# One written list for a fused attention and gated unit: VectorE turns q and k for four heads at once, the gated unit works on 512 tokens, the last 64 tokens go in 64-column halves

## The chip, the core and the metric

The kernel runs on one core of a Trainium2 chip. The core has a matrix engine (TensorE, "PE" in the profile, with its weight loads as "PEld"), three elementwise engines (VectorE "DVE", ScalarE "ACT", GpSimd "POOL"), a queue engine for transfers (SyncE "SP") and sixteen DMA engines. On-chip data lies in SBUF, with 128 partitions. Matmul results lie in PSUM, which this kernel uses as eight banks of 128 partitions by 512 fp32 values. Each engine works through its own list of instructions in order and waits at semaphores for the others. The metric is the time of one execution on the device in microseconds (us); the profile page gives the span from the first to the last instruction of one execution.

## What is computed

Two stages follow one another. The first is block-causal attention over 8 batches, 8 heads, 576 tokens and 64 dims (blocks of 64 tokens, nine of them). The second is a gated unit over the 512 channels that the heads make together.

```python
# q, k, v: (8, 8, 576, 64) fp32
scores = matmul(q, k^T) / sqrt(64);  keep where query block >= key block (blocks of 64)
x      = softmax(scores) @ v                      # then (8, 576, 512)
gate_pre[s] = sum_k conv_w[k] * x[s - 4 + k]      # five taps for each channel, causal
val  = x @ w_val                                  # 512 x 512
out  = (sigmoid(gate_pre) * val) @ w_out          # (8, 576, 512) fp32
```

The kernel takes exp without subtracting the maximum, gets each softmax sum from a column of ones beside v, and takes the sigmoid as (1 + tanh(g/2))/2, with the factor 1/2 put into w_val.

## The kernel before, in words

**Order of work.** The order is written out by hand: `PLAN` is a list of words, and `run` calls one helper for each word, so the order of the words is the order of every engine's instructions. A word such as `s.8.1@72` names a helper (`s` is `scores`), its arguments and, behind the `@`, the PSUM banks that it writes or the engine that it runs on. A short `START` list and some set-up code (ones, zeros, identity, the Exp table) come ahead of it.

**Attention.** The unit is a pair of two heads, 32 pairs in all. Of its 576 tokens the first 512 go one way and the last 64 (the tail) another.
- `load_qk` (L194) brings q and k of a pair, 256 KB each, in runs of four tokens; `load_v` brings v; `load_tails` brings the 64 tail tokens of q and k of all heads of a batch. Nearly all loads and stores are on SP's queue.
- `cast_qk` (L231) makes fp16 of q and k on GpSimd. `trans` (L263) turns them on TensorE, eight transposes of 128 x 128 for a pair, into one PSUM bank. `evac_trans` (L276) copies the bank to SBUF on VectorE and puts the tokens in order. `trans_tails` (L285) and `evac_tails` (L290) do the same for the tails.
- `scores` takes three steps `t` for a pair. In each step the two heads sit in partitions 0 to 63 and 64 to 127 of the array (64 dims each) and write 512 columns each into one bank per head. The last 64 queries are columns of step 2 with `ktails` as moving data. `exps` (L315) empties one bank, that is 512 columns, into fp16 `pts` on ScalarE. `scores_last` and `exps_last` (L327) do the tail keys of a batch. `mask` (L332, L334) zeroes the 64 x 64 blocks that the mask forbids, on GpSimd.
- `av` has one bank for a head: five query blocks of 128 (the last block has 64 real queries beside columns that are not used), each the sum over its key blocks, with `pts` as weights and v (with its column of ones) as moving data: 15 matmuls of 65 columns. `norm` (L357, L358) divides on VectorE. `xtrans` (L365) makes five transposes for a pair, and `evac_x` (L371) writes 576 tokens into `xts`.

**Gated unit.** The unit is half a batch, 288 tokens, 16 in all. `conv` makes 80 matmuls of 32 x 32 weights (the taps as diagonals `DG`), in sixteen positions of the array, into four banks; `gate` (L388) takes tanh of one bank at a time; `val` makes four products of four matmuls with 288 columns; `gated` (L402) multiplies. `proj` makes one 128-token row block of `out` from four matmuls of 512 columns (36 in all, nine for two batches), and `evac_out` (L243) copies it to `osb` on VectorE or ScalarE before `store` sends it. The last row block is split in two halves over two engines and two queues.

All matmuls but the transposes go through one helper, so their line is L133; the tiles tell them apart: `qkT` and `kt` are scores, `v,pt` and `v16t,pt` the product with v, `xt,DG` the convolution, `xt,w_val` val, `w_out,gv` proj, `ident,qk` the transposes of q and k, `ident,x` those of x.

Of the kernel before, what the change touches and what calls it, by code (L numbers as in the profile page):

```python
# [9 lines left out]

START = """
Lqk.0
"""

PLAN = """
cw@0 Lt.0 Lqk.1 Lqk.2 cq.1 cq.0 ct.0 cT w@1 w@1 w@1 w@1 w@1 w@1 w@1 w@1 tr.0@12 qkT.0 ttr.0@3 Lt.1
Lqk.3 kt.0 qka.0 Lvt.0 cq.2 w@4 w@4 s.0.0@45 e.0.0.1 s.0.1@67 e.0.0.0 s.0.2@01 Lv.0 e.0.1.0 sl.0@23
e.0.2.0 Lqk.4 w@4 tr.1@4 qkT.1 w@5 w@5 tr.2@5 Lv.1 el.0.1 e.0.1.1 ct.1 el.0.0 s.1.1@67 e.0.2.1 qkT.2
s.1.2@23 e.1.1.1 cq.3 e.1.1.0 s.1.0@40 ttr.1@1 e.1.2.1 Lqk.5 Lv.2 Lv.3 e.1.2.0 Lqk.6 w@5 s.2.1@56
Lwv.0 cvt.0 e.1.0.0 kt.1 e.1.0.1 s.2.0@71 Lwv.1 m.0 Lqk.7 w@2 tr.3@2 qkT.3 cv.0 s.2.2@30 Lt.2  # L20
e.2.1.0 e.2.0.0 m.1 cq.4 e.2.1.1 av.0.0@4 DG e.2.0.1 e.2.2.1 av.0.1@2 s.3.2@56 n.0.1 e.2.2.0 n.0.0
e.3.2.1 cv.1 s.3.1@17 e.3.2.0 tr.4@2 s.3.0@03 m.2 av.1.1@4 qkT.4 av.1.0@5 cq.5 cv.2 xtr.0@6 n.1.1
e.3.1.0 e.3.1.1 Lvt.1 s.4.0@21 e.3.0.0 Lv.4 e.3.0.1 s.4.1@74 xt.0 Lv.5 n.1.0 tr.5@6 s.4.2@03 e.4.0.1
m.3 e.4.0.0 av.2.1@5 e.4.2.1 e.4.2.0 av.2.0@1 Lqk.8 cv.3 qkT.5 n.2.1 s.5.0@26 n.2.0 e.4.1.1 e.4.1.0
cq.6 e.5.0.0 av.3.1@0 n.3.1 e.5.0.1 Lqk.9 wv.3@P av.3.0@3 Lv.7 wv.2@P xtr.1@5 sl.1@47 Lv.6 cq.7
el.1.1 el.1.0 n.3.0 s.5.1@10 xtr.2@2 xt.1 e.5.1.1 xtr.3@6 xt.2 ct.2 tr.6@3 Lqk.11 m.4 xt.3 qkT.6
e.5.1.0 Lqk.10 s.5.2@47 Lwo.3 wv.1@D cvt.1 cn.0@5260 e.5.2.1 e.5.2.0 s.6.1@13 val.0.3@4 th.0.2 cv.4
th.0.3 Lwo.2 gv.0.3 val.0.2@7 th.0.1 m.5 th.0.0 cv.5 e.6.1.1 Lwo.0 s.6.0@02 e.6.1.0 s.6.2@56 wv.0@D
tr.7@4 val.1.2@1 ttr.2@3 e.6.2.1 gv.0.2 Lwo.1 e.6.2.0 val.0.0@7 e.6.0.0 e.6.0.1 val.0.1@5 qkT.7 cq.8
s.7.1@64 gv.0.0 e.7.1.1 s.7.0@02 e.7.1.0 m.6 av.4.1@7 e.7.0.1 Lt.3 kt.2 gv.0.1 av.4.0@3 n.4.1 cq.9  # L30
s.7.2@54 e.7.0.0 e.7.2.0 av.5.1@6 n.4.0 av.5.0@7 n.5.1 Lvt.2 n.5.0 e.7.2.1 Lv.9 m.7 sl.2@02 Lv.8
xtr.4@3 el.2.1 xt.4 val.1.3@6 el.2.0 tr.8@4 cv.7 cn.1@5702 th.1.2 th.1.3 qkT.8 th.1.1 xtr.5@3 cv.6
xt.5 Lqk.13 tr.9@4 th.1.0 val.1.0@3 s.8.0@02 Lqk.12 gv.1.2 av.7.1@1 cq.11 av.6.1@5 qkT.9 e.8.0.1
gv.1.0 n.7.1 Lv.10 cq.10 s.9.2@74 wo.1@P wo.0@P e.8.0.0 s.9.1@30 n.6.1 e.9.2.0 e.9.2.1 gv.1.3
av.7.0@2 val.1.1@1 av.6.0@5 s.8.2@64 e.9.1.0 ct.3 e.9.1.1 cvt.2 n.7.0 Lqk.14 s.8.1@72 Lv.12 n.6.0
e.8.2.0 xtr.7@0 e.8.2.1 gv.1.1 e.8.1.1 xt.7 xtr.6@3 tr.11@5 s.9.0@14 xt.6 e.8.1.0 qkT.11 e.9.0.0
Lvt.3 Lv.11 tr.10@6 cn.2@0327 e.9.0.1 qkT.10 th.2.2 s.11.0@51 cv.9 val.2.2@4 o.0.1@6 gv.2.2 th.2.0
val.2.1@4 e.11.0.1 th.2.3 th.2.1 e.11.0.0 s.10.2@02 m.8 s.10.0@37 ttr.3@1 cv.8 e.10.2.1 gv.2.1
val.2.0@5 Lt.4 kt.3 e.10.0.0 e.10.2.0 o.0.0@4 Lqk.16 oc.0.1@D m.9 sl.3@10 s.10.1@26 e.10.0.1 Lqk.15
e.10.1.0 val.2.3@3 gv.2.0 el.3.1 av.8.0@5 cq.13 av.8.1@7 gv.2.3 e.10.1.1 n.8.0 n.8.1 av.9.1@3 cq.12  # L40
el.3.0 s.11.2@26 s.11.1@01 oc.0.0@D e.11.1.1 n.9.1 tr.13@5 av.9.0@7 o.0.3@4 e.11.1.0 xtr.8@0 n.9.0
xt.8 cv.10 e.11.2.1 m.10 e.11.2.0 m.11 tr.12@1 cn.3@3726 Lqk.17 qkT.12 cq.14 av.10.1@0 oc.0.3@A
Lv.15 o.0.4@4 th.3.2 tr.14@1 cv.11 th.3.0 Lv.14 qkT.13 th.3.1 th.3.3 n.10.1 qkT.14 oc.0.4@A
s.13.0@52 s.12.0@36 e.13.0.0 av.10.0@7 n.10.0 e.12.0.1 o.0.2@4 Lqk.18 s.13.1@01 e.13.0.1 cq.16
s.12.1@25 ct.4 av.11.1@7 e.12.0.0 av.11.0@3 oc.0.2@D Lvt.4 e.13.1.1 e.12.1.1 Lv.13 xtr.10@6 xtr.9@4
n.11.1 xt.10 e.13.1.0 val.3.2@7 s.13.2@01 e.12.1.0 n.11.0 st.0.0 cq.15 e.13.2.1 s.12.2@62 e.13.2.0
e.12.2.0 Lt.6 gv.3.2 e.12.2.1 cvt.3 cv.12 xt.9 xtr.11@5 xt.11 val.3.0@3 ttr.4@7 cn.4@4015 gv.3.0
val.4.0@3 th.4.0 m.12 st.0.1 val.3.1@2 th.4.1 kt.4 th.4.2 gv.4.0 tr.15@7 sl.4@63 cv.15 th.4.3 gv.3.1
Lt.5 s.14.1@01 qkT.15 el.4.0 el.4.1 s.14.2@45 val.4.2@2 av.12.1@3 val.3.3@6 e.14.1.1 Lqk.19 Lqk.20
cq.17 e.14.2.0 av.12.0@7 gv.4.2 e.14.2.1 e.14.1.0 s.14.0@24 n.12.1 gv.3.3 st.0.2 s.15.0@53 n.12.0  # L50
s.15.1@60 st.0.3 val.4.1@1 Lv.16 m.13 tr.17@7 e.14.0.0 cv.14 e.14.0.1 gv.4.1 cv.13 xtr.12@2 tr.16@4
e.15.0.0 e.15.1.1 e.15.0.1 e.15.1.0 qkT.17 xt.12 o.0.5@1 s.15.2@35 oc.0.5@D cq.18 cn.5@7062 e.15.2.1
qkT.16 e.15.2.0 th.5.3 m.14 av.13.1@1 Lv.17 Lv.19 av.13.0@3 th.5.2 val.5.1@5 n.13.1 s.16.2@41 th.5.0
th.5.1 e.16.2.1 e.16.2.0 s.16.1@02 Lqk.22 e.16.1.0 n.13.0 s.16.0@67 m.15 gv.5.1 st.0.4 av.15.1@3
av.15.0@5 xtr.13@1 n.15.1 cq.19 ct.5 val.5.0@4 Lqk.21 e.16.1.1 av.14.0@3 n.15.0 av.14.1@0 cq.20
xtr.15@2 gv.5.0 e.16.0.0 s.17.0@54 Lvt.5 e.16.0.1 s.17.1@67 n.14.0 n.14.1 val.4.3@3 xt.15 xtr.14@0
gv.4.3 e.17.0.0 tr.19@2 xt.14 cv.16 xt.13 e.17.0.1 val.5.3@4 e.17.1.0 tr.18@5 ct.6 cv.17 qkT.18
# [52 lines left out]
def kernel(  # L110
# [10 lines left out]
    nc = tc.nc  # L121
# [7 lines left out]
    NU = B // 2  # L129
# [387 lines left out]
```

## Time and profile before

| | |
|---|---|
| time of three runs | 194.16, 195.87 (median), 196.45 us |
| span of the profiled execution (its device time is not given apart from it) | 191.6 us |
| TensorE busy | 177.3 us, 93% of the span |
| VectorE busy | 136.3 us, 71% |
| ScalarE busy | 135.8 us, 71% |
| GpSimd busy | 86.7 us, 45% |
| moved by DMA | 40.43 MB, mean 211 GB/s |
| granted TensorE clock | 0.995 over the span |

A busy time is the union of an engine's instructions. A matmul's row is longer than the time that it keeps others out, because matmuls overlap: what a group of matmuls costs the engine is the distance from its start to the start of the next group. In a group row, "xN" is the number of instructions, the numbers behind the first bar are busy time in us and mean length of one in ns, and behind the second bar stands the idle time ahead of them with what ended it.

### The profile page before, as it was taken

To read this page: it belongs to the slowest core of one execution; us is meant where nothing else is said; L and a number is where in the kernel's file an instruction comes from. 1 tells how busy PE (TensorE), PEld (TensorE's weight loads), DVE (VectorE), ACT (ScalarE), POOL (GpSimd) and SP (SyncE) were. 2 spreads that over 40 slices of the span, in tenths; PEclk is the share of its full clock that TensorE was granted. 3 is DMA by queue.
4 is the path that set the end of the run, shared out by engine and by line. 5 is a ranking of instruction groups with operands and counts; after the bars stand their busy time and mean duration, and the time that the engine had idled before them with its cause. 6 is when DMAs were issued, how large, how long until landed. Compare 5 with 4: busy or idle time off the path is not lost.

```text
span 191.6 us, 8757 instructions
## 1 busy us (share of the span) xinstructions
PE 177.3 (93%) x3687; PEld 124.7 (65%) x3687; DVE 136.3 (71%) x297; ACT 135.8 (71%) x295; POOL 86.7 (45%) x171
## 2 busy tenths in 40 slices
PE   0988899999799999999998999999999999999991
PEld 0554676777558587687576676667676777875540
DVE  6325998889738987888979765967678877762630
ACT  3059999868957788884683995978788879443432
POOL 7262889963277377445447044602469061100000
PEclk9999999999999999999999999999999999999997
DMA  6999999934589999899999887999902700300756
GB/s 168 301 310 299 317 256 285 271 97 129 135 234 308 240 287 261 220 280 227 273 263 260 270 237 197 300 209 311 307 9 86 227 30 0 113 7 0 266 205 244
DMA packets 70321, 40.43 MB, mean 211 GB/s; under 512 B 48133, under 2 KB 64773, under 8 KB 70282
## 3 DMA queue, kind: packets, MB, share of 16 engines
q1 hardware_dynamic: 69328, 39.33, 71.4%
q8 instruction: 29, 0.48, 1.1%
q10 hardware_dynamic: 954, 0.53, 0.9%
q14 instruction: 10, 0.08, 0.1%
HBM read 30.42 MB, written 9.44 MB: 208 GB/s over the span
## 4 chain that ended last, share of the span: by engine, by line
PE 73%; DMA 11%; POOL 4%; DVE 4%; ACT 2%; SPq 2%; issue 2%; ACTq 0%; POOLq 0%; DVEq 0%
PE B L133 62%; DMA w_st<-in_moe_w_out_dram 7%; PE B L263 6%; PE B L365 4%; DVE qkT L276 2%; ACT pt L315 2%; DMA conv_nat<-in_moe_conv_w_dram 2%; DMA out_dram<-osb 2%; SPq L194 1%; POOL qk L231 1%; SPq L220 1%; POOL w_val L251 1%; PE B L285 1%; DVE DG L441 1%; POOL w_out L243 1%
## 5 line engine op out<-in xcount | busy, mean ns | idle before, releaser
L315 ACT ACTIVATE pt<-B 128x512 f16<-128x512 f32 x192 | 99.5, 619 | 18.5 <-PE B L133 14.6
L231 POOL CAST qk<-qks 128x1024 f16<-128x1024 f32 x31 | 32.2, 1045 | 23.6 <-DMA qks<-in_k_dram 21.5
L276 DVE COPY qkT<-B 128x1024 f16<-128x1024 f16 x31 | 37.5, 1219 | 6.7 <-PE B L263 6.5
L402 DVE SCALAR_TENSOR_TENSOR gv<-th,B 128x288 f16<-128x288 f32 x64 | 28.0, 450 | 19.2 <-PE B L133 10.0
L133 PE MATMUL B<-xt,w_val 128*128 128x288 f16 x256 | 39.4, 287 | 0.2
L133 PE MATMUL B<-w_out,gv 128*128 128x512 f16 x144 | 35.3, 379 | 1.3 <-POOL w_out L243 1.3
L133 PEld LDWEIGHTS <-pt 128*128 128x128 f16 x960 | 33.1, 97 | 5.1 <-issue 2.6
L133 PE MATMUL B<-v,pt 128*128 128x65 f16 x896 | 35.2, 194 | 0.6 <-POOL v L234 0.3
L358 DVE TENSOR_TENSOR x<-B,rc 128x320 f16<-128x320 f32 x64 | 31.5, 492 | 2.2
L388 ACT ACTIVATE th<-B 128x288 f32<-128x288 f32 x64 | 21.5, 427 | 11.9 <-PE B L133 11.9
L332 POOL MEMSET pt<- 64x384 f16 x32 | 13.6, 424 | 35.7 <-ACT pt L315 34.8
L133 PE MATMUL B<-qkT 64*128 64x128 f16 (+3 forms) x256 | 28.9, 300 | 0.5 <-DVE qkT L276 0.4
L133 PEld LDWEIGHTS <-w_val 128*128 128x128 f16 x256 | 22.4, 98 | 8.2 <-issue 2.4
L133 PEld LDWEIGHTS <-qkT 64*128 64x128 f16 x512 | 15.1, 94 | 13.2 <-issue 5.7
L234 POOL CAST v<-vst 128x512 f16<-128x512 f32 x32 | 20.2, 639 | 7.3 <-DMA vst<-in_v_dram 4.5
L133 PEld LDWEIGHTS <-gv 128*128 128x128 f16 x144 | 13.2, 98 | 13.2 <-issue 1.5
L263 PE MATMUL B<-ident,qk 128*128 128x128 f16 x256 | 20.2, 222 | 0.8 <-DVE x L358 0.7
L263 PEld LDWEIGHTS <-qk 128*128 128x128 f16 x256 | 16.3, 99 | 5.6 <-issue 3.6
L243 ACT COPY osb<-B 128x512 f32<-128x512 f32 x19 | 11.2, 593 | 12.0 <-PE B L133 11.2
L133 PE MATMUL B<-xt,DG 32*32 32x288 f16 x1280 | 17.3, 288 | 0.9 <-issue 0.9
L357 DVE RECIPROCAL rc<-B 128x5 f32<-128x5 f32 x64 | 12.0, 188 | 8.2 <-PE B L133 7.5
L133 PEld LDWEIGHTS <-DG 32*32 32x32 f16 x1280 | 12.0, 88 | 5.7 <-issue 3.3
(51 smaller groups left out, 136.4 us busy)
## 6 DMA issues: line engine op xcount, KB each, us to landing
out_dram<-osb SPq DMA_DIRECT2D x35, 256.0 KB, 3.5
qks<-in_q_dram SPq DMA_DIRECT2D x32, 256.0 KB, 4.0
vst<-in_v_dram SPq DMA_DIRECT2D x64, 128.0 KB, 4.2
qks<-in_k_dram SPq DMA_DIRECT2D x31, 256.0 KB, 4.5
tlst<-in_q_dram SPq DMA_DIRECT2D x8, 128.0 KB, 5.7
vtst<-in_v_dram SPq DMA_DIRECT2D x8, 128.0 KB, 4.7
w_st<-in_moe_w_val_dram SPq DMA_DIRECT2D x2, 512.0 KB
w_st<-in_moe_w_out_dram SPq DMA_DIRECT2D x4, 256.0 KB
```

Source lines behind the costliest of these rows:

```text
L133: nc.tensor.matmul(out=out, lhsT=lhsT, rhs=rhs, start=start, stop=stop, skip_group_check=True)
L231: nc.gpsimd.tensor_copy(out=o, in_=s)
L234: nc.gpsimd.tensor_copy(out=v16s[p % NV][0:128, 0:4, 0:2, 0:64], in_=vst[p % NVS][0:128])
L243: (eng.copy if eng is nc.scalar else eng.tensor_copy)(out=o, in_=i)
L263: nc.tensor.transpose(out=f16(m[i * (len(m) - 1)])[:, o:o + 128], in_=t[0:128, c, 2 * i:2 * i + 2, 0:64], identity=ident16[0:128, 0:128])
L276: nc.vector.tensor_copy(out=o[0:128].rearrange("p i (s n) -> p i s n", n=4), in_=f16(m[0]).rearrange("p (i n s) -> p i s n", i=2, n=4))
L315: nc.scalar.activation(out=pts[p % NPT][0:128, h, 512 * t:512 * t + 512], in_=f32(bank["s", p, t][h]), func=AF.Exp, bias=0.0, scale=0.125)
L332: nc.gpsimd.memset(pt[64:128, 0:2, 0:1536].rearrange("p h (t s) -> p h t s", t=3)[:, :, :, 0:64], 0.0)
L357: nc.vector.reciprocal(out=rc[0:128], in_=O[:, :, 64:65])
L358: nc.vector.tensor_tensor(out=x16[p % NX16][0:128, 0:5, h, 0:64], in0=O[:, :, 0:64], in1=rc[0:128].to_broadcast([128, 5, 64]), op=ALU.mult)
L388: nc.scalar.activation(out=ths[n % NTH][0:128, r, 0:288], in_=f32(bank["cn", n][r])[:, 0:288], func=AF.Tanh, bias=0.0, scale=0.5)
L402: nc.vector.scalar_tensor_tensor(out=gvs[u % 2][0:128, x, bi, hf, 0:288], in0=ths[n % NTH][0:128, x, 0:288], scalar=1.0, in1=f32(bank["val ...
```

## The change

- **q and k** are loaded for four heads of a batch (a "quad" `Q`, 16 in all) and all 576 tokens at once: partition 32h + s holds 18 tokens of head h, 4608 bytes in one run. The cast to fp16 (GpSimd, mostly) puts two tokens side by side (`[n, d, 2]`: the pair of fp16 values is one 32-bit word), so it writes with a step of two elements. `turn` then lets VectorE transpose 32 x 32 blocks of 32-bit words, SBUF to SBUF: 576 words per partition in one instruction, written with a step of nine words. No transposes of q, k on TensorE, no copy out of PSUM, no separate tails of q, k. The first quad is cast and turned in two parts.
- **Scores**: each head holds 32 partitions, the 64 dims come as two halves that are summed in PSUM; a step writes 512 columns for four heads into four banks, as two passes of four matmuls with 32-row weights. `exps` takes two banks (1024 columns) at once. The tail queries are columns of the same tiles.
- **av** has two banks for a pair and four query blocks for a head, 20 matmuls; `norm` takes both heads at once. **The tail** is worked out once for a batch: `av_tail` puts two heads in the two 64-column halves of the array, 40 matmuls with 64-column weights; `norm_tail`, `xtrans_tail`, `evac_xtail` follow.
- **Gated unit**: 512 tokens of a batch at once (units 0 to 7), and two units (8, 9) of 256 tokens from the tails of four batches each; tanh takes two banks at once. x lies in one tile `X` with six slots. Each unit has its own row blocks in `proj` (still 36).
- **w_out** is loaded as it lies and put in order by sixteen matmuls (`wp`) and two copies (`we`), in place of loads in rearranged runs.
- **One list**: `START` and the set-up code become words of `PLAN`; casts carry their engine in the word. PSUM is one tile of eight banks. The last row block is not split.

The core of the diff:

```diff
-    qks = ring(NQS, [128, 2, 2, 256], fp32, "qks")
-    qkT = ring(NQT, [128, 2, 512], fp16, "qkT")
-    pts = ring(NPT, [128, 2, 1664], fp16, "pt")
+    stage = [ring(NST, [128, 9, 2, 64], fp32, t) for t in ("qst", "kst")]
+    half = [ring(N16, [128, 9, 64, 2], fp16, t) for t in ("q16", "k16")]
+    qTs = ring(NT, [128, 2, 576], fp16, "qT")
+    kTs = ring(NT, [128, 2, 640], fp16, "kT")
+    pts = ring(NPT, [128, 4, 1536], fp16, "pt")
...
+    def load_q(Q, m, i=0):
+        b, g = divmod(Q, 2)
+        eng = nc.scalar if m == "A" else nc.sync
+        eng.dma_start(out=stage[i][Q % NST][0:128].rearrange("p n e d -> p (n e d)"),
+                      in_=(q, k)[i][b, 4 * g:4 * g + 4].rearrange("h (p t) d -> (h p) (t d)", t=18))
...
+    def cast_qk(Q, i, m, part=(0, 9)):
+        a, e = part
+        copy(ENG[m], half[i][Q % N16][0:128, a:e].rearrange("p n d e -> p n e d"),
+             stage[i][Q % NST][0:128, a:e])
...
-    def trans(p, m):
-            for c in range(4):
-                nc.tensor.transpose(out=f16(m[i * (len(m) - 1)])[:, o:o + 128], ...
-    def evac_trans(p, m, parts=(0, 1)):
+    def turn(Q, i, m, part=(0, 9)):
+        a, e = part
+        src = half[i][Q % N16][0:128, a:e].rearrange("p n d e -> p n (d e)").bitcast(fp32)
+        dst = (qTs, kTs)[i][Q % NT][0:128, 0:2, 0:576].bitcast(fp32)
+        nc.vector.transpose(out=dst.rearrange("p h (s n) -> p n h s", n=9)[:, a:e],
+                            in_=src.rearrange("p n (h s) -> p n h s", h=2))
...
+    def score(Q, m, work, o=0):
+        qt, kt = qTs[Q % NT], kTs[Q % NT]
+        for (c, j, a, e) in work:
+            for dh in range(2):
+                for h in range(4):
+                    hp = slice(32 * h, 32 * h + 32)
+                    mm(f32(m[h])[:, o + c:o + c + e - a], kt[hp, dh, 128 * j:128 * j + 128],
+                       qt[hp, dh, a:e], start=(dh == 0), stop=(dh == 1))
+
+    WORK = [[(0, 0, 0, 512)], [(0, 1, 128, 576), (448, 4, 512, 576)],
+            [(0, 2, 256, 576), (320, 3, 384, 576)]]
...
-    def exps(p, t, h, m):
+    def exps(Q, t, h, m):
+        i, j = bank["s", Q, t][2 * h:2 * h + 2]
+        nc.scalar.activation(out=pts[Q % NPT][0:128, 2 * h:2 * h + 2, 512 * t:512 * t + 512],
+                             in_=two(i, j), func=AF.Exp, bias=0.0, scale=0.125)
...
+    def av_tail(b, m):
+        bank["at", b] = m[0]
+        for g in range(2):
+            Q = 2 * b + g
+            for h in range(2):
+                c = 65 * (2 * g + h)
+                for j in range(5):
+                    for r in range(2):
+                        a = 2 * r + h
+                        if j == 0:
+                            l = pt3[b % 2][0:128, 2 * a + g]
+                        else:
+                            l = pts[Q % NPT][0:128, a, off[j] + 512:off[j] + 576]
+                        w = v16t[b % 2][0:128, 4 * g + a, 0:65] if j == 4 else \
+                            v16s[(2 * Q + r) % NV][0:128, j, h, 0:65]
+                        mm(f32(m[0])[64 * r:64 * r + 64, c:c + 65], l, w,
+                           start=(j == 0), stop=(j == 4))
...
-                    mm(f32(m[row])[cs, 0:288], DG[rs, 5 * g + kk, 0:32],
-                       xts[b % NX][rs, g, kk + 288 * hf:kk + 288 * hf + 288],
+                    mm(psv(f32(m[row])[cs], n), DG[rs, 5 * g + kk, 0:32], tokens(n, rs, g, kk),
                        start=(kk == 0), stop=(kk == 4))
...
+    def gate(n, h, m):
+        i, j = bank["cn", n][2 * h:2 * h + 2]
+        w = width(n)
+        nc.scalar.activation(out=ths[...][0:128, 2 * h:2 * h + 2, 0:w], in_=two(i, j)[:, :, 0:w],
                              func=AF.Tanh, bias=0.0, scale=0.5)
```

Two stretches of the new list, its start and its end:

```
Lv.1.0 Lq.0@A wz pads padk Lk.0 cb.0.1@P cb.0.0@D w@0 w@0 w@0 id Lq.1 w@0 w@0 Lk.1 Lk.2 w@0 w@0 w@0
...
o.9.0@4 o.9.1@0 oc.7.0@A o.7.2@6 st.7.0 oc.7.1@D st.7.1 oc.9.0@D st.9.0 oc.9.1@D st.9.1 oc.7.2@A
st.7.2
```

More of the change, by code (lines that the diff above doesn't have):

```diff
@@ L182 @@
     bank = {}
     def f32(i):
[L185 removed]
+        return PS[0:128, i]
     def f16(i):
[L188 to L203 removed]
@@ L413, in evac_out @@
[L413 to L427 removed]
+        w = width(n)
@@ new lines @@
+    OPS = {
+        "Lq": load_q, "Lk": load_k, "Lv": load_v, "Lvt": load_vtail, "Lwv": load_w_val,
+        "Lwo": load_w_out, "Lcw": load_conv, "c": cast_qk, "ca": cast_qk_a, "cb": cast_qk_b,
+        "cv": cast_v, "cvt": cast_vtail, "wv": scale_w_val, "wo": cast_w_out, "wp": order_w_out,
+        "we": evac_w_out, "T": turn, "Ta": turn_a, "Tb": turn_b, "s": scores, "e": exps,
+        "sl": scores_last, "el": exps_last, "m": mask, "av": av, "n": norm, "xtr": xtrans,
+        "xt": evac_x, "at": av_tail, "nt": norm_tail, "xtt": xtrans_tail, "xtl": evac_xtail,
+        "cn": conv, "th": gate, "val": val, "gv": gated, "o": proj, "oc": evac_out,
+        "st": store, "cw": taps, "cT": evac_taps, "DG": diags, "w": warm, "wz": zero_wz,
+        "tab": table, "id": identity, "pads": pads, "padk": pad_k,
+    }
```

563 lines of the change are left out of this document (246 added, 317 removed).

## The prediction

> **What bounds the kernel now.** I read the busy shares first, then the busy times by stretch, then the time line of TensorE. From the page:
>
> ```profile
> PE 177.3 (93%) x3687; PEld 124.7 (65%) x3687; DVE 136.3 (71%) x297; ACT 135.8 (71%) x295; POOL 86.7 (45%) x171
> ...
> PE 73%; DMA 11%; POOL 4%; DVE 4%; ACT 2%; SPq 2%; issue 2%; ACTq 0%; POOLq 0%; DVEq 0%
> ```
>
> TensorE has 93% of the span and 73% of the chain that ended last. The next view gives length, busy time (and count) of PE, PEld, DVE, ACT, POOL, clock, DMA share and GB/s for four stretches; behind it, pieces of the chain of waits at both ends of the run (start, length, what).
>
> ```profile
> 10.00:20.00 10.00, 8.55 (x116) 5.54 (x114) 4.60 (x6) 7.96 (x17) 4.93 (x9) 1.00 1.11 302
> 20.00:40.00 20.00, 19.02 (x435) 14.53 (x432) 18.12 (x41) 19.22 (x43) 16.89 (x26) 1.00 0.94 265
> ...
> 60.00:160.00 100.00, 98.49 (x2228) 71.13 (x2226) 78.81 (x170) 79.29 (x175) 48.28 (x90) 1.00 0.79 222
> 160.00:186.50 26.50, 26.50 (x476) 17.07 (x473) 14.93 (x39) 12.60 (x29) 1.11 (x4) 1.00 0.28 102
> ```
> ```profile
> 4.65 5.36 PE B L133 x16
> 10.01 0.85 PE B L263 x8
> ...
> 169.03 17.44 PE B L133 x248
> ...
> 186.50 0.44 DVE olast L243
> ```
>
> Real work on TensorE starts at 10.0 us (dummy matmuls before), ends at 186.5, and 5.1 us of last copies and stores follow. From 60 us on TensorE is full while VectorE and ScalarE have a fifth of their time free. From 20 to 40 ScalarE is as full as TensorE (19.2 of 20). So: TensorE bounds, with ScalarE beside it early.
>
> What a matmul group costs is the distance to the next start on the time line:
>
> ```profile
> 48.10 0.61 PE L263 MATMUL B<-ident,qk 128*128 128x128 f16 x8
> 48.65 0.39 PE L133 MATMUL B<-qkT 64*128 64x512 f16 x2
> 48.97 0.62 PE L263 MATMUL B<-ident,qk 128*128 128x128 f16 x8
> 49.52 1.05 PE L133 MATMUL B<-xt,DG 32*32 32x288 f16 x80
> 50.50 0.39 PE L133 MATMUL B<-qkT 64*128 64x512 f16 x2
> ...
> 54.39 0.28 PE L133 MATMUL B<-kt,qkT 64*128 64x64 f16 x8
> 54.51 0.38 PE L133 MATMUL B<-qkT 64*128 64x512 f16 x2
> 54.82 0.40 PE L285 MATMUL B<-ident,tl 128*128 128x128 f16 x4
> 55.05 0.65 PE L133 MATMUL B<-xt,w_val 128*128 128x288 f16 x4
> 55.54 0.81 PE L133 MATMUL B<-w_out,gv 128*128 128x512 f16 x3
> ```
> ```profile
> 59.92 0.59 PE L133 MATMUL B<-v,pt 128*128 128x65 f16 x14
> 60.35 0.19 PE L133 MATMUL B<-v16t,pt 128*128 128x65 f16 x1
> 60.38 1.02 PE L133 MATMUL B<-w_out,gv 128*128 128x512 f16 x4
> 61.24 0.44 PE L365 MATMUL B<-ident,x 128*128 128x128 f16 x5
> 61.52 0.61 PE L263 MATMUL B<-ident,qk 128*128 128x128 f16 x8
> ```
>
> Four proj matmuls of 512 columns take 60.38 to 61.24, 0.86: 0.215 each. Five transposes take 0.28: 0.056 each. Eight would be 0.45, but the eight ahead of a score step or a convolution take 0.55 (48.10 to 48.65): leaving full-array work for tiles costs some 0.1, and so does the way back, since a step of 512 columns takes 0.32 (48.65 to 48.97), not 0.215. The two heads of a step run side by side (both within that 0.32). Fifteen matmuls of av take 0.46: 0.029 to 0.03 each. A convolution takes 0.98, four val matmuls 0.49, eight score matmuls of 64 columns 0.12 (54.39 to 54.51).
>
> **TensorE, part by part** (both switches counted with the tiled work).
> - Transposes of q, k: 32 x 0.45 + 8 x 0.22 = 16.2 before (54.82 to 55.05 is a tail group), nothing after.
> - Scores: before 96 steps x (0.215 + 0.2) = 39.8. After 48 steps, each two passes of 512 columns by four heads: 48 x (0.43 + 0.2) = 30.2. Tail keys: 16 matmuls at 0.015 to 0.02 a batch plus switches, 0.5; 4 after, 2.6 before.
> - av: 960 x 0.029 = 27.8 before; 640 x 0.029 = 18.6 after, plus the tail. No row shows 64-column weights; bounds are 0.0145 each (two halves side by side) and 0.058 (half the pace of the full ones). I take the row itself, 0.029: 8 x (40 x 0.029 + 0.2) = 10.9 (6.2 to 20.2).
> - Transposes of x: 160 x 0.056 = 9.0, then 144 x 0.056 = 8.1.
> - Convolution: 16 x (0.98 + 0.1) = 17.3. After, five rounds with 224 columns more, 0.094 each: 8 x 1.55 + 2 x 1.0 = 14.4.
> - val 64 x 0.49 = 31.4, then 128 x 0.215 + 32 x 0.108 = 31.0. proj 31.0 both. Taps and the ordering of w_out: 1.5.
>
> Before: 175, against the 176.5 between 10.0 and 186.5, so the method accounts for the run. After: 150. The cover of the moved set-up words (ones, zeros, identity, the Exp table) is the wait for the first loads, up to 10.0 us, as now.
>
> **The other engines.** Rows of the view by group:
>
> ```profile
> L315 ACT ACTIVATE pt<-B 128x512 f16<-128x512 f32 x192 | 99.5, 619 | 18.5 <-PE B L133 14.6 <-POOL pt L334 1.0 <-issue 0.9
> ...
> L276 DVE COPY qkT<-B 128x1024 f16<-128x1024 f16 x31 | 37.5, 1219 | 6.7 <-PE B L263 6.5
> ...
> L231 POOL CAST qk<-qks 128x1024 f16<-128x1024 f32 x31 | 32.2, 1045 | 23.6 <-DMA qks<-in_k_dram 21.5 <-PE B L133 1.6
> L358 DVE TENSOR_TENSOR x<-B,rc 128x320 f16<-128x320 f32 x64 | 31.5, 492 | 2.2
> L402 DVE SCALAR_TENSOR_TENSOR gv<-th,B 128x288 f16<-128x288 f32 x64 | 28.0, 450 | 19.2 <-PE B L133 10.0 <-ACT th L388 6.9 <-ACT pt L315 2.0
> ...
> L388 ACT ACTIVATE th<-B 128x288 f32<-128x288 f32 x64 | 21.5, 427 | 11.9 <-PE B L133 11.9
> ...
> L234 POOL CAST v<-vst 128x512 f16<-128x512 f32 x32 | 20.2, 639 | 7.3 <-DMA vst<-in_v_dram 4.5 <-PE B L133 1.8
> ...
> L371 DVE COPY xt<-B 128x576 f16<-128x576 f16 x32 | 13.9, 450 | 1.3 <-PE B L365 0.7 <-ACT pt L315 0.5
> ...
> L332 POOL MEMSET pt<- 64x384 f16 x32 | 13.6, 424 | 35.7 <-ACT pt L315 34.8
> ...
> L357 DVE RECIPROCAL rc<-B 128x5 f32<-128x5 f32 x64 | 12.0, 188 | 8.2 <-PE B L133 7.5 <-ACT pt L315 0.3
> ...
> L243 ACT COPY osb<-B 128x512 f32<-128x512 f32 x19 | 11.2, 593 | 12.0 <-PE B L133 11.2 <-ACT olast L243 0.5
> L243 DVE COPY osb<-B 128x512 f32<-128x512 f32 x16 | 10.9, 688 | 5.9 <-DMA out_dram<-osb 2.9 <-PE B L133 2.9
> ...
> L334 POOL MEMSET pt<- 64x128 f16 x32 | 6.4, 200 | 0.0
> ...
> L327 ACT ACTIVATE pt<-B 128x256 f16<-128x256 f32 x16 | 5.9, 408 | 0.5 <-PE B L133 0.5
> ...
> L251 POOL TENSOR_SCALAR w_val<-w_st 128x512 f16<-128x512 f32 x2 | 3.0, 1500 | 0.0
> ```
>
> - ScalarE: 512 columns occupy it for 99.5/192 = 0.518, and 256 more columns add (619 - 408) = 0.211, so 1024 occupy it for 0.94. 96 exps 90.2, 16 of 256 columns 4.9, 16 + 4 gates 17.1, two copies of w_out 2, 13 output copies 6.5: 121.
> - VectorE: a turn is 576 words. The copy at L276 reads PSUM with a step of 128 elements at 1.04 ns an element plus 0.15; so 0.755, 30 whole turns and two in parts, 24.2. Its writes have a step of 36 bytes, which no row shows: up to twice per element, 1.355. norm 32 x (0.19 + 0.69), tails 5 + 2.3, xt 32 x 0.42, gated 32 x 0.68 + 8 x 0.42, 23 output copies 15.9, the rest 4: 118.
> - GpSimd: 1152 elements from 639 and 1045: 1.15 a cast, 28 of them 32; v 20.4, v tails 5, masks 17, weights 8: 84. The step of two elements in the write is not in the trace; bounds 1.15 and, at the 2.93 ns an element of L251 (1500/512), 3.37. I take 1.15, the same operation.
>
> **The sum.** Up to the last exp of the sixth quad the list holds 38 us for ScalarE (36 exps of 0.94, six of 0.31, two gates), but for TensorE only 26: 18 steps 11.3, eight av 4.6, two tails 2.7, seven transposes of x 1.6, tail keys 1.5, one convolution 1.55, two val 1.7, the taps 0.9. The gated unit starts no earlier. The loads that this stretch needs are 7.1 MB of q and k, 3.1 of v, 2.1 of weights and the tails, near 13 MB: 45 us at 290 GB/s, between the 302 and 265 of the two early stretches above. So two limits lie near 48 us after a start at 10, which I leave where it is: the first quad loads twice the bytes, but no transposes and copies stand ahead of its scores. I take 49. SP has 32 loads of q and k where there were 79 with the tails, in one queue with the stores; a store that waits for its copy still holds the loads behind it, as now, so I cost it at nothing; if loads came late the stretch at 265 GB/s would be 49 us long, not 45.
>
> Then 124 on TensorE, and 5.1 for the last copy and store, plus 0.2 as the last block isn't split (0.593 for a whole copy in place of the 0.44): 178. That TensorE waits no more after 49 us is what the trace shows now; but the seventh quad holds some 10 us on each of four engines, for which I add 1. Behind the last exp, av of the last two pairs waits for a mask of 1.07 (768 and 256 elements by the slope from 200 to 424 ns at L334 and L332) that was 0.62; ahead of it in TensorE's order stand one av, three val or proj and four transposes, 3.4 us, against 1.98 + 1.07 for exps and mask: covered by 0.3. Span 179. The median run lies 4.3 above the profiled span (195.87 - 191.6), the lowest 2.6: **179 + 4 = 183**. What no longer counts is the copy at L276; what is late next is ScalarE early, then TensorE again.
>
> [...]
> [...]
>
> **Rivals.**
> - *The turn costs 1.355.* VectorE goes to 137 and is the fullest in a few quads (13 in the seventh): taking the fullest engine quad by quad, the sum rises by 6.6. **190**. Chance 0.13.
> - *PSUM banks (slower).* A step now takes four of eight banks at once and ScalarE gives them back in two pairs, the last 1.98 us after the step (1.04 + 0.94); before, two banks after 0.62 + 0.52 = 1.14. TensorE works in order: a group behind the step whose bank is not free stops everything. Price: the 0.8 difference at half of 48 steps, 20 us: **203**. It undoes the change from 0.27 a step on (13/48). For it: no row has such steps. Against it: from 60 to 160 us PE lost 1.5 of 100. Chance 0.11.
> - *GpSimd's casts at 3.37.* 62 us more, 146 in all, the fullest engine in nine quads, which adds 25 if it can run ahead and 35 if not: **208 to 218**. Chance 0.06.
> - *The change does not do what it says:* four heads run three at a time (0.43 x 4/3, 0.14 x 48 = 6.9 more: **190**, chance 0.05) or two (0.43 x 48 = 20.6 more: **203**, chance 0.03).
> - *Better:* tail matmuls two at a time (-4.7) and loads no slower than ScalarE in the first quads (-1), the seventh quad without loss (-1): **176**. Chance 0.10.
>
> **How the numbers follow.** Forecast 0.52, 178 to 188. No change of under 1% (about what a measurement of this kernel can tell, 194 to 198) lies only at the foot of the slow cases: 0.04. Slower by more: 0.19. Faster: 0.77. The range reaches from the better case, less 6 for the error of the stretch up to 49 us (half of the 12 by which ScalarE exceeds TensorE there), to the bank rival: 170 to 203; what is left out is the GpSimd case and the far ends.
>
> **What would show it.** Right: no `ident,qk` group; turns near 0.76; exps of 1024 columns near 1.04; a score step 0.6 from start to start; 40 tail matmuls in about 1.3; TensorE busy near 160, ScalarE near 121. Wrong: idle time of PE released by ACT or DVE (banks), GpSimd busy over 110 (casts), turns over 1.2, or the last exps later than 150 us.

## The result: slower by a third

The changed kernel takes 258.82 us (median of four, 258.46 to 261.28) against 196.03 us for the kernel before (194.16 to 196.45): ratio 1.340, 95% interval 1.325 to 1.354. The forecast was 183 us with a range of 170 to 203. For each set of runs below the kernel before was run again beside it; ratios are to that kernel, both without the executions that ran some per cent slower at a lower clock, while medians and ranges hold all executions.

Busy times, the chain that ended last, and the clock in 40 slices, from the page of the changed kernel (span 257.1 us, its own run 258.83 us):

```profile
PE 188.5 (73%) x3015; PEld 106.1 (41%) x3015; DVE 129.3 (50%) x232; ACT 128.1 (50%) x150; POOL 90.2 (35%) x127
...
PEclk9855556757999997799958979995558999769999
...
PE 45%; ACT 14%; DVE 14%; issue 4%; POOL 1%; ACTq 0%; DVEq 0%
PE PS L103 42%; ACT pt L271 10%; DVE x L329 5%; PE PS L343 3%; DVE gv L406 2%; DVE osb L197 2%; ACT th L388 2%; DVE rc L328 1%; DVE kT L244 1%; POOL w_val L223 1%; DVE qT L244 1%; ACT w_out L197 1%; ACT pt L281 1%; DVE X L349 0%; PE PS L354 0%
```

No engine is full. TensorE stands for 27% of the span where it stood for 7%, and the other engines are half idle. This is not an engine that has too much to do: the chain goes back and forth between TensorE, the exps (L271) and the norm (L329). The granted clock, 0.995 on average before, is 0.826.

Groups of the same kernel, shapes kept apart (line, engine, operation, count, busy us, mean ns, idle before):

```profile
L271 ACT ACTIVATE pt<-PS 128x1024 f16<-128x1024 f32 x96 | 94.0, 1023 | 67.7 <-PE PS L103 51.5 <-DVE x L329 6.3 <-DVE gv L406 4.7
...
L197 POOL CAST k<-kst 128x1152 f16<-128x1152 f32 x14 | 20.6, 1479 | 9.2 <-DVE gv L406 5.9 <-DVE kT L244 3.1
...
L244 DVE STREAM_TRANSPOSE qT<-q 128x576 f32<-128x576 f32 x15 | 18.1, 1209 | 3.0 <-POOL q L197 2.9
L244 DVE STREAM_TRANSPOSE kT<-k 128x576 f32<-128x576 f32 x15 | 18.1, 1204 | 0.0
```

The exps are as long as forecast (1.02 us); turn and cast are longer (1.21 and 1.48 us). But look at the idle time of the exps: ScalarE waits 6.3 us for the norm and 4.7 us for the gated product, both VectorE's work. An exp needs nothing from either of them. So these waits look like waits for a place, not for a result, and PSUM is the place that an exp, a norm and a gated product share.

The waits of the changed kernel (us in total, times, longest):

```profile
PEld L103 <- issue: 86.7, 152, 3.0
ACT pt L271 <- PE PS L103: 51.5, 38, 7.2
DVE rc L328 <- PE PS L103: 33.4, 17, 5.4
PE PS L103 <- ACT pt L271: 28.5, 26, 3.6
...
PE PS L103 <- DVE x L329: 12.0, 14, 2.8
```

TensorE waits for exps (28.5 us) and for norms (12.0 us), as one expects where PSUM banks are scarce. Which bank does it wait for? The list has `av.1@57 n.1` and shortly behind it `s.2.2@2346`: the product with v of pair 1 goes into banks 5 and 7, norm `n.1` empties them, and a score step writes banks 2, 3, 4 and 6. On the time line:

```profile
30.59 0.11 PEld L103 LDWEIGHTS <-kT 32*128 32x128 f16 x4
30.60 0.45 PE L103 MATMUL PS<-qT,kT 32*128 32x320 f16 x3
30.77 0.21 DVE L328 RECIPROCAL rc<-PS 128x8 f32<-128x8 f32 x1 [0.89 <-PE PS L103]
31.02 0.69 DVE L329 TENSOR_TENSOR x<-PS,rc 128x512 f16<-128x512 f32 x1
31.54 0.61 POOL L197 CAST v16t<-vtst 128x512 f16<-128x512 f32 x1
31.62 1.22 DVE L244 STREAM_TRANSPOSE kT<-k 128x576 f32<-128x576 f32 x1
31.76 1.01 PE L103 MATMUL PS<-qT,kT 32*128 32x320 f16 x13 [0.71 <-DVE x L329]
```

Three matmuls start at 30.60, into banks 2, 3 and 4. The fourth, into bank 6, starts at 31.76, just behind the end of the norm (31.02 + 0.69 = 31.71), which reads banks 5 and 7. Bank 6 lies between them. In the trace this matmul waits for VectorE's semaphore, which the norm raises at its end, so the wait stands in the program. The norm reads both banks with one instruction through this view:

```python
def two(i, j):
    return PS[0:128, i:j + 1:j - i]      # banks i and j: a step of j - i banks
```

PSUM is one tile of eight banks in this kernel (the kernel before has eight tiles of one bank), and the program's waits seem to take such a view as everything from i to j. A second place, with the list's words `s.8.0@0126`, `xtr.12@4 xt.12`, `e.8.0.1`, `cn.2@0135`, VectorE, ScalarE and TensorE from the time line:

```profile
103.53 0.39 PE L103 MATMUL PS<-X,DG 32*32 32x512 f16 x2
104.02 1.19 DVE L244 STREAM_TRANSPOSE qT<-q 128x576 f32<-128x576 f32 x1
105.07 0.40 DVE L349 COPY X<-PS 128x512 f16<-128x512 f16 x1
105.50 1.02 ACT L271 ACTIVATE pt<-PS 128x1024 f16<-128x1024 f32 x1 [2.14 <-DVE X L349]
106.58 1.09 PE L103 MATMUL PS<-X,DG 32*32 32x512 f16 x32 [2.66 <-ACT pt L271]
```

The exp reads banks 2 and 6 and waits until VectorE has copied x out of bank 4, and that copy stands behind a turn. The convolution has written two banks and waits for the exp, because its third, bank 3, lies between 2 and 6. Nobody uses what the other makes, and TensorE stands for 2.66 us.

Matching the list word by word with the trace, I compared each first write into a bank with the last read of that bank and the last read that only passes over it. For 97 first writes the passing read ended later than the bank's own; not one of them started before it had ended. In 46 places this cost TensorE over 0.1 us, together 58.4 us (35.9 behind exps, 14.8 behind norms, 4.8 behind the last exps, 2.8 behind gates and w_out). That count runs from the start of the matmul ahead of the wait. The profile's idle time, from the end of that matmul, is 49.9 us in 44 places; waits for banks that were really in use have 7.7 us of idle time. The kernel before reads one bank with each exp (128x512 at L315), so it has no such view there.

### The profile page after: what moved, and what is told of

Same layout as the page of the kernel before. It is cut to its first block, busy times and chain, and to the rows that moved or that the text cites. A ratio compares the mean times of both kernels' runs of the same rounds, so it can differ in the third digit from the quotient of the medians.

```text
span 257.1 us, 7008 instructions
## 1 busy us (share of the span) xinstructions
PE 188.5 (73%) x3015; PEld 106.1 (41%) x3015; DVE 129.3 (50%) x232; ACT 128.1 (50%) x150; POOL 90.2 (35%) x127
## 4 chain that ended last, share of the span: by engine, by line
PE 45%; ACT 14%; DVE 14%; issue 4%; POOL 1%; ACTq 0%; DVEq 0%
PE PS L103 42%; ACT pt L271 10%; DVE x L329 5%; PE PS L343 3%; DVE gv L406 2%; DVE osb L197 2%; ACT th L388 2%; DVE rc L328 1%; DVE kT L244 1%; POOL w_val L223 1%; DVE qT L244 1%; ACT w_out L197 1%; ACT pt L281 1%; DVE X L349 0%; PE PS L354 0%
## 5 line engine op out<-in xcount | busy, mean ns | idle before, releaser
L271 ACT ACTIVATE pt<-PS 128x1024 f16<-128x1024 f32 x96 | 94.0, 1023 | 67.7 <-PE PS L103 51.5
L103 PE MATMUL PS<-qT,kT 32*128 32x64 f16 (+4 forms) x768 | 47.0, 333 | 23.8 <-DVE x L329 8.2
L103 PE MATMUL PS<-w_out,gv 128*128 128x512 f16 x144 | 40.5, 414 | 11.0 <-ACT pt L271 7.9
L103 PE MATMUL PS<-v,pt 128*128 128x65 f16 (+1 forms) x896 | 38.6, 214 | 12.8 <-ACT pt L271 9.3
L103 PEld LDWEIGHTS <-pt 128*128 128x128 f16 (+1 forms) x960 | 35.3, 117 | 22.1 <-issue 14.6
L103 PE MATMUL PS<-X,w_val 128*128 128x512 f16 (+1 forms) x160 | 38.6, 374 | 1.5 <-ACT pt L271 1.5
L406 DVE SCALAR_TENSOR_TENSOR gv<-th,PS 128x512 f16<-128x512 f32 (+1 forms) x40 | 27.3, 690 | 20.1 <-PE PS L103 9.6
L197 POOL CAST k<-kst 128x1152 f16<-128x1152 f32 (+2 forms) x16 | 22.3, 1397 | 13.3 <-DVE gv L406 5.9
L329 DVE TENSOR_TENSOR x<-PS,rc 128x512 f16<-128x512 f32 x32 | 22.1, 691 | 1.1
L197 POOL CAST q<-qst 128x1152 f16<-128x1152 f32 x14 | 20.5, 1474 | 0.1
```

The lines of the kernel that those rows point to most:

```text
L103: nc.tensor.matmul(out=out, lhsT=lhsT, rhs=rhs, start=start, stop=stop, skip_group_check=True)
L197: (eng.copy if eng is nc.scalar else eng.tensor_copy)(out=o, in_=i)
L271: nc.scalar.activation(out=pts[Q % NPT][0:128, 2 * h:2 * h + 2, 512 * t:512 * t + 512], in_=two(i, j), func=AF.Exp, bias=0.0, scale=0.125)
L329: nc.vector.tensor_tensor(out=x16[P % NX16][0:128].rearrange("p i h d -> p h i d"), in0=O[:, :, :, 0:64], in1=rc[0:128].to_broadcast([128, ...
L406: nc.vector.scalar_tensor_tensor(out=o, in0=i0, scalar=1.0, in1=i1, op0=ALU.add, op1=ALU.mult)
```

## The experiments

**Theory A:** the waits for passed-over banks make the change slow. **Rival B:** the banks are scarce by themselves, four to a step of eight. **Rival C:** turns and casts are too slow and feed TensorE late.

### Banks side by side

The list's bank numbers are chosen anew; no word is moved and no helper is changed.

```diff
-... av.1@57 ... s.2.2@2346 ... s.8.0@0126 ... xtr.12@4 ... cn.2@0135 ...
+... av.1@67 ... s.2.2@0145 ... s.8.0@4501 ... xtr.12@6 ... cn.2@2345 ...
```

> The changed kernel with other bank numbers in its list, so that the two banks which one instruction reads always stand side by side (i, i+1); order of the work and all instructions are the same. Theory A (waits for banks that are only passed over: a read of banks 5 and 7 holds back the matmuls that write bank 6): the 58 us of such waits go and with them the half clock, 190 to 210 us, granted clock over 0.9. Rival B (the banks themselves are scarce, four to a step with eight in all): the same banks are busy as long as before, 245 to 265 us. Rival C (the slow turns and casts feed TensorE too late): nothing of that changes, 250 to 260 us.

Measured: 188.46 us (186.94 to 191.47), 0.949 of the kernel before (0.928 to 0.970). Page and waits of this kernel, and its exps from the view by group:

```profile
PE 163.3 (87%) x3015; PEld 94.6 (50%) x3015; DVE 126.5 (67%) x232; ACT 125.8 (67%) x150; POOL 90.6 (48%) x127
...
PEclk9955569699999999999998799999999999999999
```
```profile
PE PS L103 <- ACT pt L271: 5.3, 11, 1.1
...
PE PS L103 <- DVE x L329: 1.7, 6, 0.5
```
```profile
L271 ACT ACTIVATE pt<-PS 128x1024 f16<-128x1024 f32 x96 | 92.9, 1027 | 28.0 <-PE PS L103 25.1 <-issue 1.9 <-POOL v L197 0.8
```

This is a little under A's range of 190 to 210. 70 us are gone with nothing changed but bank numbers: B and C both fall as causes of the slowdown. TensorE's waits for exps go from 28.5 to 5.3 us, those for norms from 12.0 to 1.7, and the exps wait for VectorE no more. The count that gave 58.4 us gives 0.0 here, while the idle time in waits for banks in use does not fall (10.8 us, where it was 7.7).

### One bank for each read

```diff
-        i, j = bank["s", Q, t][2 * h:2 * h + 2]
-        nc.scalar.activation(out=pts[Q % NPT][0:128, 2 * h:2 * h + 2, 512 * t:512 * t + 512],
-                             in_=two(i, j), func=AF.Exp, bias=0.0, scale=0.125)
+        for a, i in enumerate(bank["s", Q, t][2 * h:2 * h + 2]):
+            nc.scalar.activation(out=pts[Q % NPT][0:128, 2 * h + a, 512 * t:512 * t + 512],
+                                 in_=f32(i), func=AF.Exp, bias=0.0, scale=0.125)
```

The same was done to the last exps, the gate, the norm and the copies of w_out.

> The changed kernel with the bank numbers of its list as they are, but every read of two banks (exps, last exps, gate, norm, the two copies of w_out) split into two reads of one bank each. Theory A: no read spans a bank that isn't its own, so the 58 us of waits go, while ScalarE gets about 125 and VectorE about 64 more instructions at an unmeasured fixed price each, say 0.1 to 0.2 us: 200 to 220 us. Rivals B (scarce banks) and C (turns and casts): 255 to 285 us, because ScalarE and VectorE only get more to do.

Measured: 187.45 us (185.96 to 188.73), 0.947 (0.924 to 0.970). The old bank numbers are harmless once no read spans two banks, so B falls with the same numbers too. The time lies below A's range of 200 to 220, because the price of the added instructions was put too high. From its page:

```profile
PE 165.5 (89%) x3015; PEld 97.0 (52%) x3015; DVE 132.6 (72%) x296; ACT 133.1 (72%) x284; POOL 90.5 (49%) x127
```

134 more instructions on ScalarE add 7.3 us to the 125.8 with adjacent banks (0.054 each), 64 on VectorE 6.1 (0.095 each). TensorE is the fullest engine in both kernels. So reading two banks at once, a part of the change, shows no gain in these runs; the two kernels differ in bank numbers as well, and one-bank reads with adjacent banks were not tried.

### Which reader

Two kernels with the changed kernel's own bank numbers: in one only exps and last exps were split as above, in the other only the norm.

> The changed kernel with its own bank numbers; only the exps and the last exps read one bank each, the other reads of two banks stay. Theory A: of the 58.4 us of waits for passed-over banks that the trace of the changed kernel shows, 35.9 end with an exps and 4.8 with a last exps; these go, and at the rate of the kernel with adjacent banks (70 us of time for 58 us of waits) that is 49 us: 200 to 222 us, median about 210. If the exps were only the place where another shortage shows, the waits would move to the norms: over 235 us.

> The changed kernel with its own bank numbers; only the norm (reciprocal and multiply) reads one bank at a time, the exps stay. Theory A: 14.8 of the 58.4 us of waits for passed-over banks end with a norm; they go at the same rate of 70 to 58, less some for 64 more instructions on VectorE: 236 to 250 us, median about 242. If the norm alone were the cause: under 215 us.

Measured: 213.06 us (212.99 to 213.72) and 239.63 us (239.58 to 239.95). Exps alone give back 45.8 us, norms alone 19.2. Together that is 65.0 of the 70.4 us between 258.82 and 188.46. The forecasts of A, from the share of each reader in the 58.4 us, were 210 and 242. Of the 49.9 us of idle time in waits for passed-over banks 15.0 and 40.7 us are left in these two kernels.

### Banks far apart

```diff
-... av.1@57 ... s.2.2@2346 ... s.8.0@0126 ... xtr.12@4 ... cn.2@0135 ...
+... av.1@37 ... s.2.2@1405 ... s.8.0@1526 ... xtr.12@7 ... cn.2@0415 ...
```

> The changed kernel with other bank numbers, so that the two banks of every pair lie three or more apart: 166 pairs pass over 513 banks, where those of the changed kernel pass over 138 and those of the kernel with adjacent banks over none. Order and instructions are the same. Theory A: more matmuls meet a read that passes over their bank, 275 to 320 us. Rivals: if the number of banks or their order of use decides, 245 to 265 us.

> The bank numbers of the kernel with pairs far apart, but every read takes one bank. Theory A: the distance of the two banks has no effect any more, 187 to 203 us. If far banks are worse by themselves (they fall free in a worse order), over 215 us.

Measured: 374.05 us (373.41 to 376.13) and, with the same numbers but one bank for each read, 200.33 us (199.75 to 200.47). Clock and waits with banks far apart:

```profile
PEclk9655555555558667855568689988957669766999
```
```profile
ACT pt L271 <- PE PS L103: 81.4, 41, 7.2
PE PS L103 <- ACT pt L271: 64.2, 48, 2.6
...
ACT pt L271 <- DVE x L329: 29.5, 8, 6.7
```

The more banks a pair passes over, the longer the run: 0, 138 and 513 passed-over banks give 0, 49.9 and 114.8 us of idle time in such waits and medians of 188.46, 258.82 and 374.05 us. A had expected at most 320, so the effect was underrated, not its direction. The second kernel shows that these numbers are worse in themselves by 12.9 us (200.33 against 187.45), so the other 173.7 us between 374.05 and 200.33 come with reading two banks at once.

### Turn and cast without steps

```diff
-        copy(ENG[m], half[i][Q % N16][0:128, a:e].rearrange("p n d e -> p n e d"),
+        copy(ENG[m], half[i][Q % N16][0:128, a:e].rearrange("p n d e -> p n (d e)")
+             .rearrange("p n (e d) -> p n e d", e=2),
...
-        nc.vector.transpose(out=dst.rearrange("p h (s n) -> p n h s", n=9)[:, a:e],
+        nc.vector.transpose(out=dst.rearrange("p h (n s) -> p n h s", n=9)[:, a:e],
```

> The changed kernel with its casts of q and k written without the step of two elements and its turns written without the step of nine words; this leaves out the order of the tokens and of the two halves of d, so the scores are those of other tokens. Turn and cast fall towards 0.75 and 1.15 us. Theory A: these two are not what the kernel waits for, 245 to 258 us. Rival C (turns at 1.2 and casts at 1.48 us are the cause of the 63 us): 32 turns give back 14 us and 32 casts 10 us directly, and more by the clock: 195 to 230 us.

> Both edits together: banks side by side, and casts and turns written without steps (the order of the tokens and halves is left out). It tells what the slow turns and casts cost once the waits for passed-over banks are gone. Theory A with a bound by TensorE behind it: within 4 us of the kernel with adjacent banks alone, 188 to 206 us. Rival C in a weak form (they cost once the rest is gone): 8 to 20 us less than with adjacent banks alone, 175 to 192 us.

Measured: 257.40 us (256.08 to 258.40) with the changed kernel's bank numbers, 185.04 us (184.48 to 185.40) with banks side by side. Groups of the first of these kernels:

```profile
L197 POOL CAST k<-kst 128x1152 f16<-128x1152 f32 x14 | 16.2, 1161 | 10.3 <-DMA kst<-in_k_dram 10.2
...
L245 DVE STREAM_TRANSPOSE qT<-q 128x576 f32<-128x576 f32 x15 | 11.5, 767 | 3.1 <-POOL q L197 3.0
```

Without the steps turn and cast take 0.767 and 1.161 us, the forecast's 0.755 and 1.15. Where the false waits rule, this gives 1.4 us, less than the spread of either set (256.08 to 258.40, and 258.46 to 261.28). With them gone it gives 3.4 us by the medians, and the intervals of the two ratios overlap (0.934, 0.923 to 0.945, against 0.949, 0.928 to 0.970). Rival C fails in its strong form. In its weak form it forecast 8 to 20 us less, and A up to 4, so the difference is A's; the time itself, 185.04, lies in C's range and under A's, since the kernel with adjacent banks was faster than A had it.

### Which of the two, and a moved list

Three kernels with adjacent banks ran beside a repeat of the first one. In one only the turn lost its step; in another the cast runs in the order of what it writes:

```diff
-        copy(ENG[m], half[i][Q % N16][0:128, a:e].rearrange("p n d e -> p n e d"),
-             stage[i][Q % NST][0:128, a:e])
+        copy(ENG[m], half[i][Q % N16][0:128, a:e],
+             stage[i][Q % NST][0:128, a:e].rearrange("p n e d -> p n d e"))
```

In the last, many words of the list stand earlier or later, with adjacent banks throughout and the same 811 words.

> The kernel with adjacent banks once more, beside the three others of this call, which are read against it: 186 to 191 us.

> The kernel with adjacent banks, its turns written without the step of nine words (this leaves out the order of the tokens), its casts as they were. It tells whether the 3.4 us between the kernels with adjacent banks with and without steps belong to the turn or to the cast. If to the turn, which my forecast sized at 0.755 us and which takes 1.21: 184.5 to 186.5 us. If to the cast on GpSimd: 187.5 to 189.5 us.

> The kernel with adjacent banks, its casts of q and k run in the order of what they write (neighbouring words out, a step of 64 words in) instead of the order of what they read; the same numbers end in the same places. If the step on the writing side is what takes 1.48 instead of 1.15 us: the cast falls to 1.15 to 1.3 us and the time by 0 to 2 us. If the step costs the same on the reading side: cast 1.48 us or longer, time as before within 1 us.

> The kernel with adjacent banks, with some of its words moved in the list and the adjacent banks chosen anew; the same instructions. The trace with adjacent banks shows TensorE busy for 28.7 us of its first 40 and for 94% of the time after that, so that there is little left to gain by order alone: 182 to 188 us if the moves fill some of the early waits, 188 to 192 us if not.

Measured, with the ratio to the kernel before:

| kernel | median us (six runs) | ratio, 95% interval |
|---|---|---|
| adjacent banks, again | 187.62 (186.25 to 189.88) | 0.969 (0.964 to 0.975) |
| turn without step | 185.57 (184.73 to 187.75) | 0.959 (0.953 to 0.964) |
| cast in the order of its writes | 186.88 (186.11 to 188.45) | 0.968 (0.961 to 0.974) |
| moved words | 191.95 (189.74 to 193.74) | 0.989 (0.979 to 0.999) |

The turn's step is worth about 2.0 us (the two intervals still touch). The cast in the other order takes 1.41 instead of 1.49 us, between the two forecasts and too little to be seen in the time. The moved list lost 4.3 us, where it was meant to fill early waits: the miss of this set. Of the kernels that do the whole work, those with adjacent banks in the changed kernel's order and the one with one-bank reads and its bank numbers are the fastest, 3 to 5% faster than the kernel before.

## Why the prediction was wrong, by its own steps

- **The step that failed** is in the sum: "That TensorE waits no more after 49 us is what the trace shows now". The trace of before showed it for reads of one bank each; I carried it over to reads of two banks, with other banks in between, and never looked at the view that makes them. In the changed kernel the last exp of the sixth quad ends at 68.91 us, not at 49. Behind it TensorE is busy for 139.1 of 188.2 us, so it stands for 49 us where I had allowed 1:

```profile
0.00:68.91 68.91, 49.38 (x741) 29.26 (x745) 32.94 (x60) 40.71 (x46) 35.76 (x55) 0.68 0.84 241
68.91:257.10 188.19, 139.07 (x2296) 76.81 (x2273) 96.39 (x173) 87.37 (x104) 54.49 (x72) 0.88 0.42 126
```

- **The bank rival** (203 us, chance 0.11) named the right resource with the wrong mechanism. It priced how late a bank in use is given back. Those waits have 7.7 us of idle time in the changed kernel and 10.8 with adjacent banks, where the run is faster than before. What was not on the list were waits for banks that nobody uses. The signs that I had named for it ("idle time of PE released by ACT or DVE") did appear, and would have been read as scarce banks: only the bank number of the waiting matmul tells the two apart.
- **The rest of the forecast** can be read from the kernel with adjacent banks, which is the change without the false waits: 188 us for 183. Its stretches (length, busy PE, PEld, DVE, ACT, POOL, clock, DMA share, GB/s, as in the two lines above), cut at the end of the last exp of the sixth quad and 5.1 us before the end:

```profile
0.00:54.16 54.16, 41.65 (x741) 24.73 (x745) 32.09 (x60) 40.01 (x46) 35.75 (x55) 0.81 1.00 293
54.16:182.50 128.34, 120.65 (x2294) 69.63 (x2271) 93.74 (x172) 85.17 (x104) 54.88 (x72) 0.99 0.61 182
182.50:187.60 5.10, 1.02 (x5) 0.29 (x3) 0.71 (x2) 0.59 (x1) 0.00 (x0) 0.97 0.57 213
```

- *The early stretch:* 49 us forecast, 54.2 measured. ScalarE's own work was right: from its first exp at 12.94 us it is busy for 37.8 us, where I had 38. What was put too low is the start, 10 us, and the 3.4 us that ScalarE waits behind it. The loads came at 293 GB/s, close to the 290 that I had taken.
- *TensorE behind it:* 124 us of work and 1 of waits forecast; 120.7 busy and 7.7 idle measured. Here too "waits no more" was too bold, by 7 us, and half of that was made up by work that was put too high.
- *The time around the span:* 4.3 us forecast. The profiled run of this kernel took 189.41 us for a span of 187.6, so 1.8, and so did the runs of the kernel before that have both numbers (1.7 to 2.0); the rest of the 4.3 was the distance of the profiled execution from the median. The distance from 183 to 188 is the sum of these errors of both signs, so it is partly luck that it is no larger.
- *The terms of the sum,* on TensorE's time line of the same kernel:

```profile
44.19 0.44 PE L103 MATMUL PS<-v,pt 128*64 128x65 f16 x8
...
45.07 0.63 PE L103 MATMUL PS<-qT,kT 32*128 32x448 f16 x16
45.70 0.61 PE L343 MATMUL PS<-ident,x 128*128 128x128 f16 x8
46.67 0.77 PE L103 MATMUL PS<-v,pt 128*128 128x65 f16 x20 [0.36 <-DVE X L349]
47.37 0.61 PE L103 MATMUL PS<-qT,kT 32*128 32x512 f16 x8
47.91 0.39 PE L103 MATMUL PS<-X,DG 32*32 32x512 f16 x2
...
53.30 1.35 PE L103 MATMUL PS<-X,DG 32*32 32x512 f16 x80
54.58 1.04 PE L103 MATMUL PS<-X,w_val 128*128 128x512 f16 x4
```

A score step takes 0.63 (45.07 to 45.70) or 0.54 (47.37 to 47.91), at or under the 0.63 of the forecast: four heads do run side by side, since 0.54 is less than the 0.573 that three at a time would take without any switch (8 x 0.215/3, an estimate from the 0.215 of the prediction's rows), and the rivals with three or two at a time (0.77 and 1.06 by the forecast's sum) fall. A tail takes 0.88 (44.19 to 45.07) where I had 1.36: 64-column matmuls cost 0.022 each, between the row that I took and the better case. An av takes 0.70 where I had 0.58, a convolution 1.28 where I had 1.55.
- *The turn* takes 1.21 us, near the upper bound of 1.355, whose factor of two was my guess, and not the 0.755 that I took. The step of 36 bytes is the reason, since without it the turn takes 0.767. The 0.755 took over the pace of L276, which reads with wide steps, but the prediction's own rows show twice the pace for neighbouring values: L371 copies 576 fp16 in 0.450 us, 0.52 ns an element above the same 0.15 (the copies of 512 and 256 columns at L243 of the kernel before, 0.688 and 0.425 us, give 0.16), against 1.04 at L276; whether the step is the reason there, no run tells. The cost of the turn's step, 2.0 us, is far below the 6.6 of the rival, since VectorE, at 67%, doesn't bound.
- *The cast* takes 1.48 us, not 1.15; the step of two elements costs 0.32. The rival at 3.37 falls.
- *The other engines* have 128.1 (ScalarE), 129.3 (VectorE) and 90.2 us (GpSimd) in the changed kernel, where I had 121, 118 and 84 (the terms that I gave for GpSimd add up to 82.4).

How the loss splits is shown only in part. Between the two spans, 257.1 and 187.6 us, lie 69.5 us: TensorE is idle for 44.3 us more in the changed kernel, and busy for 25.2 us more (188.5 against 163.3) with the same instructions, while the mean clock was 0.826 in place of 0.935. What the low clock costs by itself was not tried apart.

## What to carry to other kernels

When an instruction reads two places of a shared tile with a step, ask what the program's waits make of the places between; put such pairs side by side or read them one by one. (A tile for each bank, as the kernel before has it, was not tried in the changed kernel.) When an engine waits for another whose result it doesn't need, write down which bank or buffer each of the two touches before calling the buffers scarce. A claim that an engine never waits holds for the reads, banks and order in which it was seen.

## What the runs showed of the hardware

**In the trace of the changed kernel the granted clock changes in steps of 3.41 us.** Stretches of it (length, busy PE first, clock third from the end):

```profile
37.64:41.05 3.41, 1.28 (x38) 1.00 (x35) 3.03 (x4) 1.70 (x5) 3.22 (x4) 1.00 0.88 327
41.05:44.47 3.42, 2.30 (x31) 1.33 (x28) 1.75 (x3) 2.74 (x3) 1.72 (x3) 0.50 0.41 89
44.47:47.88 3.41, 3.28 (x45) 2.11 (x43) 1.68 (x5) 1.02 (x1) 0.00 (x0) 0.50 0.38 137
170.77:174.19 3.42, 1.08 (x35) 0.85 (x25) 1.38 (x4) 1.02 (x1) 3.30 (x6) 1.00 1.04 307
174.19:177.60 3.41, 2.28 (x12) 0.97 (x15) 0.32 (x1) 1.02 (x1) 1.15 (x1) 0.50 0.02 9
191.26:194.67 3.41, 3.10 (x24) 1.38 (x23) 1.01 (x3) 0.58 (x1) 0.37 (x1) 0.50 0.00 0
194.67:198.08 3.41, 2.56 (x94) 1.55 (x88) 0.34 (x1) 1.94 (x2) 0.00 (x0) 1.00 0.03 7
```

A window at full clock in which TensorE was busy for 1.28 or 1.08 us is followed by windows at exactly half; a window at half that was busy for 3.28 or 3.10 us is followed by full clock, though another of 3.11 us (54.71 to 58.12) was not. Cutting the whole run from 10.33 us on in this way, windows at full clock with up to 1.42 us of work were always followed by half clock, those from 1.7 us on never, and in between both happened. Another trace blurs this edge: with adjacent banks a full-clock window with 2.04 us of work (30.26 to 33.67) was followed by half. Between 174.19 and 194.67 six windows in a row ran at half, with 1.8 to 3.1 us of busy time each. The work ahead of that stretch is spread out, but no pause is as long as a window (the longest, 2.23 us, ends at 175.32); TensorE's time line there:

```profile
172.33 0.77 PE L103 MATMUL PS<-v,pt 128*128 128x65 f16 x20 [1.25 <-ACT pt L271]
175.32 1.01 PE L103 MATMUL PS<-w_out,gv 128*128 128x512 f16 x2 [2.23 <-ACT pt L271]
```

Pauses of 1.25 and 2.23 us were enough here, so in this trace the busy share of a window seems to matter, not one long gap. With the waits went more time than their own length: 49.9 us of idle time in waits for passed-over banks, and 70.4 us between the medians of 258.82 and 188.46.

**In this trace a read waits for a read, at the program's semaphore.** The exp at 105.50 waited for the semaphore of a copy that only reads PSUM, with 2.14 us of idle time, and for a bank that only lay between the two that it read. Which part of the software put this wait in is not shown.
